# Sliding-window attention followed by a swish feed-forward layer: a second table for the order of all operations, the engine choices, the PSUM slots and the idle products

## The chip, the core and the metric

The kernel runs on one core of a Trainium2 chip. The metric is device microseconds of one execution; lower is better. The core has a matmul engine (PE, with PEld for its weight loads), a vector engine (DVE), a scalar engine (ACT), a general engine (POOL) and a queue that issues most of the DMA transfers (SP). Each engine works through its own list of instructions in order and waits where an input or a buffer is not there yet.

## What is computed

Attention over 4 batches, 8 heads, 768 positions and 64 columns a head, then a feed-forward layer on the 3072 rows that come out of it. Three heads (0, 2 and 6) are causal over all earlier keys. The other five see only the first 4 keys ("sink") and a window of the last 64.

```python
scores = q @ k.T / sqrt(64)              # per batch and head
keep   = causal                          # heads 0, 2, 6
keep   = causal & (is_sink | in_window)  # heads 1, 3, 4, 5, 7
a      = softmax(where(keep, scores, -1e9))
x      = (a @ v).reshape(3072, 512)
h      = x @ w_in                        # 512 -> 2048
g      = h * sigmoid(beta * h)
out    = g @ w_out                       # 2048 -> 512
```

Inputs and output are float32; the products run on bfloat16 copies.

## The kernel before, in words

**Units.** The work is cut into 8 units: batch `b` (0 to 3) by half of the sequence `u` (0, 1), 384 positions each, numbered n = 2b + u. For each unit the kernel does the following; the names are those of the code and of the tiles.

- Loads of q and k (`load_qk`, a transfer of 192 KB for two heads, tiles q2f and k2f; for units 4 to 7 `load_block`, three transfers into a wf tile) and of v (`load_v`, vf or wf).
- Casts to bfloat16 (`cast_qk`, `cast_block` into c; `cast_v` into vb) and shifted or patched copies of v (`shift_v`, `sink_v`: vs, vb; `cast_edge`: VE).
- Transposes of q and k to columns: for units 0 to 3 as products with an identity on PE (`transposes_of`, `transposes`) with a copy out of PSUM (`qk_copy`, tile QK), for units 4 to 7 as DMA transposes (`turn_block`). `kp_copy` and `qd_copy` prepare more copies of k and q (KP, and a k2f tile).
- Scores (`scores`, PSUM tiles sp and b), exponentials on ACT (`exps`, tile es), masks (`masks`), row sums as products with one-hot columns (`sums`, `sums_d`, PSUM tile b) and products with v (`pv`, PSUM tile sp).
- For units 0 and 1 the reciprocals of the sums are spread by products on PE (`recips`, `split`, `spread`, `norm_held`). For units 2 to 7 they are turned and spread by DMA: `sums_copy` moves the sums to tile sc, `sums_turn` transfers them to rec, `recips_d` takes the reciprocal there (DVE RECIPROCAL rec), `spread_w` writes them to device memory (rd), `spread_r` reads them back into tile R, two transfers of 384 KB for an even unit, and for an odd one two of 192 KB, one of 384 KB and a small one. `norm` then multiplies the products with v by R into xT.
- The feed-forward layer: 16 up-steps of four products (`mm1`, xT by w_in into a b bank, 384 columns), a tanh on ACT (`swish_a`, tile t, 2 buffers) and a multiply on DVE (`swish_b`, tile gT), then 48 down-products (`mm2`, gT by w_out, 512 columns) in three groups of 16 with a copy out (`out_copy`, tile osb, 3 buffers) and a store each (`out_store`). The last 128 rows of unit 7 are done in two parts of 384 and 128 columns (`mm2_last`, `last_copy`, `last_store`).

The weights w_in and w_out come in four transfers of 1 MB each into wf (`load_w_in`, `load_w_out`, 3 buffers of wf, shared with the later loads) and are cast by POOL in four pieces each (`cast_w_in`, `cast_w_out`). The up-steps of unit 0 need the first w_in transfer.

**What sets the order.** Every operation is entered once with `plan.add` (1109 of them: engine or engines it may run on, what it needs and gives, which PSUM slot it takes or drops). The entered costs are not used any more: `_Plan.run` goes through the table `SEQUENCE`, which lists the operations' numbers, and emits them one after the other. So each engine's order is the order of its operations in that table. Where an operation may run on several engines, the string `CHOICE` says which ("a" ACT, "d" DVE, "g" POOL). The string `SLOTS` says which of the 4 single PSUM banks (b) or the 2 double banks (sp) an operation takes. `_Ordered` keeps the emitted order.

**Idle products.** `fill` puts products whose result nobody reads ahead of the real ones into a bank that is about to be written: `fill_first` 25 of them at the very start (input blank, an xT tile of zeros), and the table `FILLS` says how many before which operation of the first units (products of blank, or transposes of the identity where the bank is a bfloat16 one).

Of the kernel before, what the change touches and what calls it, by code (L numbers as in the profile page):

```python
# [38 lines left out]


SEQUENCE = [
# [51 lines left out]
]  # L93
CHOICE = (
    "daagaddadadddadaddaddgggdgdddgaaaggggggaaagdddaddaddagddddgaaddgddaaadagddadadagggggadggagdgggagggdd"
    "gaadaaadaaadaaadaadaadaaaada"
)
SLOTS = (
    "0120130120131210031201100312010312132301201031210032103101230012031203120312310231010210310210231021"
    "0301100101201013021302130210130211031001201032100123012301230123001200131230120130123012310021013203"  # L100
    "01130012103210013201320132100023102301231212310231001230123012301230210"
)


# [1 line left out]
    return bass.AP(ap.tensor, ap.offset + offset, [list(ap.ap[0])] + dims)  # L106


FILLS = {24: 4, 28: 8, 32: 1, 36: 1, 45: 5, 51: 7, 54: 5, 60: 1}


class _Ordered:
# [60 lines left out]
def kernel(  # L173
# [1260 lines left out]
    for i, f, e in plan.run():  # L1434
        held["fill"] = FILLS.get(i, 0)
        f(e)
# [35 lines left out]
```

## Time and profile before

| what | us |
|---|---|
| median of 3 runs (lowest to highest) | 229.29 (228.82 to 229.96) |
| span of the profiled execution | 227.1 |
| the median less the span | 2.2 |
| PE busy, share of the span | 220.0 (97%) |
| DVE busy | 152.0 (67%) |
| ACT busy | 144.4 (64%) |
| POOL busy | 97.1 (43%) |

The span goes from the first to the last instruction of one profiled execution; the runs' time contains what lies around it too. The trace has no time of the profiled execution other than its span, so the difference of 2.2 us to the median is taken for what lies around it. A busy PE counts each product from its start to its modelled end, so a short pause between two products does not show as idle; the distance from the start of one product to the start of the next does show it. "L123" in the rows is the line of the recording helper `_Ordered`, the same for all; the tiles tell the operations apart. In a row of the timeline stand the start, the time that the merged instructions took, the engine, the operation, the tile written and those read, the shapes, the count, and in brackets the idle time before it and what ended that.

### The profile page before, as it was taken

To read this page: it belongs to the slowest core of one execution; us is meant where nothing else is said; L and a number is where in the kernel's file an instruction comes from. 1 tells how busy PE (TensorE), PEld (TensorE's weight loads), DVE (VectorE), ACT (ScalarE), POOL (GpSimd) and SP (SyncE) were. 2 spreads that over 40 slices of the span, in tenths; PEclk is the share of its full clock that TensorE was granted. 3 is DMA by queue.
4 is the path that set the end of the run, shared out by engine and by line. 5 is a ranking of instruction groups with operands and counts; after the bars stand their busy time and mean duration, and the time that the engine had idled before them with its cause. 6 is when DMAs were issued, how large, how long until landed. Compare 5 with 4: busy or idle time off the path is not lost.

```text
span 227.1 us, 6564 instructions
## 1 busy us (share of the span) xinstructions
PE 220.0 (97%) x2595; PEld 127.2 (56%) x2595; DVE 152.0 (67%) x391; ACT 144.4 (64%) x244; POOL 97.1 (43%) x238
## 2 busy tenths in 40 slices
PE   7688999999999999999999999999999999999995
PEld 7564567664545565555654665465655555456543
DVE  5787988888292878856862668983796864157700
ACT  6899979886447488616786198318965665118620
POOL 5528966965978108749566293042800000000000
PEclk9999999999999999999999999999999999999999
DMA  6999999998999969999999996947801027021012
GB/s 185 283 321 369 242 343 349 371 335 217 233 205 244 213 131 235 270 176 208 267 219 189 202 214 192 219 26 178 188 0 46 4 89 200 3 92 46 3 46 92
DMA packets 84264, 42.28 MB, mean 186 GB/s; under 512 B 66042, under 2 KB 77002, under 8 KB 84234
## 3 DMA queue, kind: packets, MB, share of 16 engines
q1 hardware_dynamic: 83962, 41.67, 76.7%
q8 instruction: 20, 0.33, 0.6%
q10 hardware_dynamic: 272, 0.20, 0.3%
q14 instruction: 10, 0.08, 0.1%
HBM read 32.27 MB, written 6.37 MB: 170 GB/s over the span
## 4 chain that ended last, share of the span: by engine, by line
PE 87%; DMA 5%; DVE 3%; ACT 2%; SPq 1%; issue 1%; POOL 0%; ACTq 0%
PE b L123 77%; PE sp L123 10%; DMA vf<-in_v_dram 3%; DMA q2f<-in_q_dram 2%; DVE gT L123 1%; ACT t L123 1%; SPq L123 1%; ACT R L123 1%; DVE vs L123 1%; DVE xT L123 0%; ACT vb L123 0%; DVE QK L123 0%; POOL c L123 0%; DVE b L123 0%; DVE lo L123 0%
## 5 line engine op out<-in xcount | busy, mean ns | idle before, releaser
L123 PE MATMUL b<-xT,w_in 128*128 128x384 bf16 x512 | 89.9, 326 | 0.1
L123 PE MATMUL b<-w_out,gT 128*128 128x512 bf16 (+2 forms) x400 | 88.3, 371 | 0.0
L123 DVE SCALAR_TENSOR_TENSOR gT<-t,b 128x384 bf16<-128x384 f32 x128 | 68.5, 551 | 26.2 <-ACT t L123 22.5
L123 ACT ACTIVATE t<-b,beta_h 128x384 f32<-128x384 f32 x128 | 72.2, 586 | 18.3 <-PE b L123 9.7
L123 PEld LDWEIGHTS <-w_in 128*128 128x128 bf16 x512 | 48.6, 98 | 33.4 <-issue 0.6
L123 PEld LDWEIGHTS <-gT 128*128 128x128 bf16 x400 | 37.4, 98 | 40.9 <-issue 0.8
L123 ACT ACTIVATE es<-sp 128x1024 bf16<-128x1024 f32 (+2 forms) x44 | 41.2, 961 | 6.5 <-PE sp L123 6.0
L123 ACT ACTIVATE osb<-b 128x512 f32<-128x512 f32 (+1 forms) x18 | 10.5, 583 | 34.7 <-PE b L123 34.7
L123 DVE TENSOR_TENSOR xT<-sp,R 64x384 bf16<-64x384 f32 (+4 forms) x31 | 16.6, 554 | 12.2 <-PE sp L123 9.2
L123 POOL CAST c<-wf 128x256 bf16<-128x256 f32 x48 | 20.7, 473 | 7.6 <-DMA wf<-in_k_dram 7.4
L123 POOL COPY KP<-QK 128x24 bf16<-128x24 bf16 (+5 forms) x41 | 9.9, 286 | 27.1 <-DMA QK<-c 16.6
L123 PE MATMUL sp<-QK 64*64 64x128 bf16 (+6 forms) x360 | 14.9, 240 | 0.9 <-ACT QK L123 0.8
L123 DVE TENSOR_TENSOR es<-es,mask_s 128x128 bf16<-128x128 bf16 (+8 forms) x34 | 13.0, 402 | 3.8 <-ACT es L123 3.6
L123 PEld LDWEIGHTS <-QK 64*64 64x64 bf16 (+1 forms) x432 | 10.8, 106 | 7.2 <-issue 4.9
L123 DVE TENSOR_TENSOR es<-es,mask_c 128x128 bf16<-128x128 bf16 (+3 forms) x42 | 10.4, 272 | 6.2 <-ACT es L123 6.1
L123 POOL CAST vb<-wf 128x512 bf16<-128x512 f32 x18 | 11.2, 629 | 7.9 <-DMA wf<-in_v_dram 7.8
L123 PE MATMUL sp<-es,vb 128*64 128x64 bf16 (+5 forms) x245 | 13.0, 233 | 0.3 <-ACT es L123 0.3
L123 ACT COPY sc<-b 128x384 f32<-128x384 f32 x5 | 2.4, 479 | 15.7 <-PE b L123 15.7
L123 DVE TENSOR_SCALAR osb<-b 128x512 f32<-128x512 f32 (+1 forms) x7 | 4.7, 667 | 11.3 <-PE b L123 11.3
L123 PEld LDWEIGHTS <-vb 128*64 128x64 bf16 x257 | 11.6, 111 | 0.7 <-issue 0.3
L123 POOL CAST w_in<-wf 128x512 bf16<-128x512 f32 x16 | 9.4, 624 | 4.7 <-DMA wf<-in_moe_w_in_dram 4.6
L123 DVE COPY QK<-b 128x384 bf16<-128x384 bf16 (+1 forms) x13 | 8.2, 640 | 4.8 <-PE b L123 4.7
(120 smaller groups left out, 212.1 us busy)
## 6 DMA issues: line engine op xcount, KB each, us to landing
out_dram<-osb SPq DMA_DIRECT2D x23, 256.0 KB, 3.6
wf<-in_v_dram SPq DMA_DIRECT2D x18, 256.0 KB, 5.3
wf<-in_moe_w_in_dram SPq DMA_DIRECT2D x4, 1024.0 KB, 8.5
wf<-in_moe_w_out_dram SPq DMA_DIRECT2D x4, 1024.0 KB
R<-rd SPq DMA_DIRECT2D x9, 384.0 KB, 5.7
q2f<-in_q_dram SPq DMA_DIRECT2D x16, 192.0 KB, 4.1
wf<-in_q_dram SPq DMA_DIRECT2D x12, 256.0 KB, 4.0
wf<-in_k_dram SPq DMA_DIRECT2D x12, 256.0 KB, 3.8
```

Source lines behind the costliest of these rows:

```text
L123: ins = f(*a, **k)
```

## The change

Four tables are replaced; no function is touched, and the operations with their needs are the same.

- `SEQUENCE`: another order of the same 1109 operations.
- `CHOICE`: 60 operations change their engine. ACT has 14 fewer, POOL 6 fewer, DVE 20 more. Of the casts of q and k for units 0 and 1, DVE has 7 instead of 3. From ACT to DVE go three copies of sums (units 2, 5 and 6), the copies of eight output blocks and of the last small part of the output (128 columns), and two casts of constants; from DVE to ACT go two output blocks and the larger last part (384 columns). Some copies out of PSUM into QK change both ways.
- `SLOTS`: other PSUM banks for the new order.
- `FILLS`: the idle products after the first 25 are dealt to other places, 29 in place of 32.

```diff
 SEQUENCE = [
-    0, 2, 467, 477, 482, 478, 14, 12, 484, 4, 6, 483, 485, 8, 486, 464, 1, 3, 470, 80, 469, 28, 82, 26, 29, 27, 10,
...
+    467, 0, 4, 477, 6, 469, 478, 5, 482, 30, 483, 1, 2, 7, 12, 3, 13, 32, 14, 484, 26, 8, 33, 10, 31, 27, 464, 80,
...
 CHOICE = (
-    "daagaddadadddadaddaddgggdgdddgaaaggggggaaagdddaddaddagddddgaaddgddaaadagddadadagggggadggagdgggagggdd"
-    "gaadaaadaaadaaadaadaadaaaada"
+    "gagdadggdggddaadadaaddgdggddddaaddgddgdagdgdddadddaadgdddddaaddddaaaadddgaddadadddggagdgdggdggdggddg"
+    "dddaaadddddaaaddaaddddaadaad"
...
-FILLS = {24: 4, 28: 8, 32: 1, 36: 1, 45: 5, 51: 7, 54: 5, 60: 1}
+FILLS = {24: 3, 28: 3, 30: 7, 45: 3, 51: 3, 54: 5, 76: 3, 104: 2}
```

What this does to an engine is read from its list of instructions. First the SP queue near the start, from the row behind the load of beta (osb) on; six loads of q and k stand ahead of beta there before, and seven now. The loads named q2f and k2f are 192 KB each, those named vf are v for unit 0, wf is the first w_in transfer and those after it. Before:

```order
L123 DMA q2f<-in_q_dram 128x2x192
L123 DMA k2f<-in_k_dram 128x2x192 x2
L123 DMA vf<-in_v_dram 128x8x64 x3
L123 DMA wf<-in_moe_w_in_dram 128x4x512
L123 DMA k2f<-in_k_dram 128x2x192
L123 DMA q2f<-in_q_dram 128x2x192 x3
L123 DMA k2f<-in_k_dram 128x2x192 x2
L123 DMA wf<-in_moe_w_in_dram 128x4x512 x2
```

And now:

```order
L123 DMA q2f<-in_q_dram 128x2x192
L123 DMA k2f<-in_k_dram 128x2x192
L123 DMA q2f<-in_q_dram 128x2x192
L123 DMA vf<-in_v_dram 128x8x64 x2
L123 DMA k2f<-in_k_dram 128x2x192
L123 DMA vf<-in_v_dram 128x8x64
L123 DMA q2f<-in_q_dram 128x2x192
L123 DMA wf<-in_moe_w_in_dram 128x4x512
L123 DMA k2f<-in_k_dram 128x2x192
L123 DMA wf<-in_moe_w_in_dram 128x4x512
```

In front of the first w_in transfer stand 12 loads of q and k on SP where there were 9 (one more is on ACT's queue in both), and the same three of v; between the first and the second w_in transfer stands one such load where there were six.

Next the SP queue around the sums of unit 2: rec<-sc is `sums_turn`, rd<-rec `spread_w`, R<-rd `spread_r`; wf<-in_v is v for unit 3, wf<-in_q and wf<-in_k are the blocks for unit 4, out_dram<-osb are stores. Before:

```order
L123 DMA wf<-in_q_dram 128x8x64 x3
L123 DMA rec<-sc 96x1x32
L123 DMA wf<-in_v_dram 128x8x64 x3
L123 DMA vf<-in_v_dram 10x8x64 x3
L123 DMA rd<-rec 96x32
L123 DMA out_dram<-osb 128x512
L123 DMA wf<-in_k_dram 128x8x64 x3
L123 DMA out_dram<-osb 128x512
L123 DMA R<-rd 64x4x384 x2
```

And now:

```order
L123 DMA wf<-in_q_dram 128x8x64 x3
L123 DMA wf<-in_k_dram 128x8x64 x3
L123 DMA vf<-in_v_dram 10x8x64 x3
L123 DMA rec<-sc 96x1x32
L123 DMA wf<-in_v_dram 128x8x64 x3
L123 DMA rd<-rec 96x32
L123 DMA_TRANSPOSE QK_109<-c 128x8x128
L123 DMA R<-rd 64x4x384 x2
```

The k blocks of unit 4 now stand ahead of the sums, two stores stand behind R, and a DMA transpose for unit 4 stands between rd and R.

Last DVE at the same place, up to the reciprocal of unit 2's sums (RECIPROCAL rec). gT is `swish_b`, QK with k2f are copies for unit 3, KP is `kp_copy`, VE and vs belong to v, es with mask_c is a mask. Before:

```order
L123 SCALAR_TENSOR_TENSOR gT<-t,b_1432 128x384
L123 COPY QK_110<-b_1572 128x2x384
L123 COPY k2f<-QK_110 64x384
L123 COPY k2f<-QK_110 64x256
L123 RECIPROCAL rec<-rec 96x32
L123 COPY QK_110<-b_1609 128x2x384
```

And now, the last twelve rows ahead of it (the copy of the sums, sc, which was ACT's, stands a few rows further up, with a copy into QK, two into k2f and three into KP between):

```order
L123 COPY KP_112<-QK_110 128x6x60
L123 COPY KP_112<-QK_110 128x6x4
L123 COPY KP_112<-QK_110 128x6x6
L123 COPY KP_113<-QK_110 128x6x60
L123 COPY KP_113<-QK_110 128x6x4
L123 COPY KP_113<-QK_110 128x6x6
L123 MEMSET VE 128x224
L123 CAST VE<-vf 30x448
L123 TENSOR_TENSOR es_1_1617<-es_1_1617,mask_c 128x2x128 x2
L123 COPY vs<-vb 64x1024
L123 MEMSET vs 64x128
L123 RECIPROCAL rec<-rec 96x32
```

The reciprocal, which stood right behind two small copies, now stands behind nine copies into KP, two rows for VE, two masks and two rows for vs.

On PE, the row sums of unit 2 stand 27 down-products and four groups of transposes later than before, the first up-step of unit 2 where it was: between the two lie 53 down-products now, and 80 with the four groups before. For unit 7 there are 27 down-products and 13 up-steps between the sums and the unit's first up-step, and 64 and 11 before. The large products (up and down) run in 37 stretches with smaller ones between, and in 39 before.

More of the change, by code (lines that the diff above doesn't have):

```diff
@@ L41 @@
 SEQUENCE = [
[51 rows of a table removed]
[51 rows of a table added]
 ]
 CHOICE = (
-    "daagaddadadddadaddaddgggdgdddgaaaggggggaaagdddaddaddagddddgaaddgddaaadagddadadagggggadggagdgggagggdd"
-    "gaadaaadaaadaaadaadaadaaaada"
+    "gagdadggdggddaadadaaddgdggddddaaddgddgdagdgdddadddaadgdddddaaddddaaaadddgaddadadddggagdgdggdggdggddg"
+    "dddaaadddddaaaddaaddddaadaad"
 )
 SLOTS = (
-    "0120130120131210031201100312010312132301201031210032103101230012031203120312310231010210310210231021"
-    "0301100101201013021302130210130211031001201032100123012301230123001200131230120130123012310021013203"
-    "01130012103210013201320132100023102301231212310231001230123012301230210"
+    "0123001213002110101101211010312010320131012013210101320110201321031203120312031203101201320132310201"
+    "0213101310101332103210320113021103210132110103101201320132013212010101023103130201102302301020132031"
+    "01231010213021032103210131001320131031031023110020320301210302302130130"
 )
```

100 rows, old and new, of the table SEQUENCE are left out of this document.

## Prediction

> **What bounds the kernel now.** I read the page first: shares of the engines, the clock, and what the transfers moved in 40 slices.
>
> ```profile
> span 227.1 us, 6564 instructions
> ...
> PE 220.0 (97%) x2595; PEld 127.2 (56%) x2595; DVE 152.0 (67%) x391; ACT 144.4 (64%) x244; POOL 97.1 (43%) x238
> ...
> PEclk9999999999999999999999999999999999999999
> ...
> GB/s 185 283 321 369 242 343 349 371 335 217 233 205 244 213 131 235 270 176 208 267 219 189 202 214 192 219 26 178 188 0 46 4 89 200 3 92 46 3 46 92
> ```
>
> PE is busy for 220.0 of 227.1 us, at full clock from the first slice on. So an order can win only where PE is idle, 7.1 us in all, or where PE's own work gets shorter. Next the busy time by stretch, in columns PE, PEld, DVE, ACT, POOL, clock, DMA share, GB/s:
>
> ```profile
> 0.00:22.50 22.50, 18.26 (x297) 13.09 (x297) 16.26 (x61) 18.67 (x32) 12.16 (x42) 1.00 0.97 289
> 22.50:224.30 201.80, 201.74 (x2300) 114.12 (x2298) 135.70 (x332) 125.44 (x212) 84.94 (x196) 1.00 0.76 176
> ```
>
> Of the 7.1 us idle, 4.24 lie in the first 22.5 us, where the transfer engines are 97% busy, and 0.06 in the 201.8 us after that; the other 2.8 are the last output's way out. From 22.5 us on PE never waits, so there a new order can only lose, but for shorter PE work. The start can win or lose. Of it I read PE's timeline:
>
> ```profile
> 18.58 0.49 PE L123 MATMUL b<-xT,w_in 128*128 128x384 bf16 x2
> 19.36 0.34 PE L123 MATMUL b<-ident,c 128*128 128x128 bf16 x3 [0.29 <-POOL c L123]
> ...
> 20.10 0.65 PE L123 MATMUL b<-xT,w_in 128*128 128x384 bf16 x3
> 20.59 0.33 PE L123 MATMUL b<-ident,c 128*128 128x128 bf16 x3
> 20.76 0.49 PE L123 MATMUL b<-xT,w_in 128*128 128x384 bf16 x2
> 21.52 0.34 PE L123 MATMUL b<-ident,c 128*128 128x128 bf16 x3 [0.27 <-DVE QK L123]
> ...
> 22.60 0.54 PE L123 MATMUL sp<-QK 64*64 64x64 bf16 x23
> ```
>
> The first up-step starts at 18.58 us; around it stand transposes of unit 1 that wait for their casts. Two up-products take 2 x 0.162 us (worked out below), so PE paused from about 18.91 to 19.36 (0.45) and from 21.09 to 21.52 (0.43). What released the first up-step is in POOL's timeline and SP's, with DVE's for xT:
>
> ```profile
> 17.54 1.17 POOL L123 CAST w_in<-wf 128x512 bf16<-128x512 f32 x2 [2.87 <-DMA wf<-in_moe_w_in_dram]
> ```
>
> ```profile
> 9.44 1.02 SPq L123 DMA_DIRECT2D wf<-in_moe_w_in_dram  x1
> ```
>
> ```profile
> 17.61 1.95 DVE L123 TENSOR_TENSOR xT<-b,R 128x384 bf16<-128x384 f32 x4 [0.40 <-PE b L123]
> ```
>
> The first w_in transfer is issued at 9.44 us and POOL, waiting for it, starts to cast at 17.54: 8.1 us for 1 MB at a time when 283 to 321 GB/s flow, so it stood behind what was queued ahead of it.
>
> **Part A, the start.** Three more q and k loads of 192 KB (0.59 MB) stand ahead of w_in. At the 283 to 321 GB/s of the second and third slice that is 1.8 to 2.1 us: w_in lands at 19.4 to 19.6 instead of 17.5, and two pieces cast in 1.17 put the first up-step at 20.5 to 20.8. How late may it be without loss? PE now does work ahead of it that came behind: by the rows above the transposes and scores from 19.36 to 20.10 (0.74), the transposes from 20.59 to 20.76 (0.17), and about 14 of the 23 small products at 22.60, some 0.2: 1.1 us. The two pauses (0.88) go too, since what they wait for is loaded sooner. So it may start at 18.58 + 1.1 + 0.9 = 20.6. Between 20.5 and 20.8 I take **+0.1**. Bounds: at the first slice's 185 GB/s the three loads cost 3.2 us, which leaves +1.2; at 369 GB/s 1.6 us, which leaves -0.4.
>
> Four casts of q and k more on DVE (0.36 us each by the row in the rivals) lie in 22.50 - 16.26 = 6.2 us of idle DVE, and POOL loses them ahead of its w_in casts; nothing, unless they land just ahead of xT (a rival). Three fewer idle products stand where PE waits anyway: nothing, and if one stood on the path it would save some 0.1.
>
> **Part B, unit 2.** Its row sums come later on PE and its first up-step doesn't. Here is PE after the sums, and the product xT that ends the way:
>
> ```profile
> 55.96 3.63 PE L123 MATMUL b<-w_out,gT 128*128 128x512 bf16 x16
> 59.42 1.17 PE L123 MATMUL b<-ident,c 128*128 128x128 bf16 x18
> 60.43 0.81 PE L123 MATMUL b<-w_out,gT 128*128 128x512 bf16 x3
> ```
>
> ```profile
> 76.65 2.60 DVE L123 TENSOR_TENSOR xT<-sp,R 64x384 bf16<-64x384 f32 x4 [0.65 <-PE sp L123]
> ```
>
> Sixteen down-products take 59.42 - 55.96 = 3.46 us, 0.216 each (and an up-product of 384 columns three quarters of it, 0.162). The room from the sums' end to xT was 76.65 - 55.96 = 20.7 us. It loses 27 x 0.216 = 5.8 and four groups of transposes, 24 products, 18 of which take 1.01 and so all 1.34: **13.5 us** are left. The chain that must fit was, on SP and DVE:
>
> ```profile
> 58.20 0.79 SPq L123 DMA_DIRECT2D rec<-sc  x1
> ...
> 63.73 0.45 SPq L123 DMA_DIRECT2D rd<-rec  x1
> ...
> 67.94 1.34 SPq L123 DMA_DIRECT2D R<-rd  x2
> ```
>
> ```profile
> 61.83 0.39 DVE L123 COPY k2f<-QK 64x384 bf16<-64x384 bf16 x2 [0.91 <-ACT QK L123]
> 62.25 0.35 DVE L123 RECIPROCAL rec<-rec 96x32 f32<-96x32 f32 x1
> 62.52 0.89 DVE L123 COPY QK<-b 128x768 bf16<-128x768 bf16 x1
> 63.44 1.12 DVE L123 COPY KP<-QK 128x360 bf16<-128x360 bf16 x9
> ...
> 66.06 0.38 DVE L123 CAST VE<-vf 30x448 bf16<-30x448 f32 x1
> ```
>
> The tile view gives the way of R from issue to landing, and SP's timeline the price of the DMA transpose that now stands ahead of R:
>
> ```profile
> DMA to landing us min/median/max: 3.4/4.4/5.7
> ```
>
> ```profile
> 81.77 1.26 SPq L123 DMA_TRANSPOSE QK<-c  x1
> ```
>
> Of the DVE work that now stands ahead of the reciprocal nearly all is the stretch from 61.83 to 66.44, 4.6 us with the reciprocal in it; with the copy of the sums (no DVE row shows it; half of QK's 0.89, an estimate: 0.4) and one more mask (0.3, likewise) it ends 5.3 us after the sums. The turn of the sums runs beside it: issued at 58.20, its result was in use at 62.25, at most 4.05 us, so it is not later than DVE. Then rd's issue, 0.45, and the transpose's, 1.26: the first R is issued at 7.0 and the second 0.67 (half of 1.34) later, at 7.7. With 4.4 us to land R is all there at 12.1, with 5.7 at 13.4; the room is 13.5. Should R wait for rd as it did before (63.73 to 67.94 = 4.2 us, with two stores and three loads between, which hide whether it waited), R goes out at 5.3 + 4.2 = 9.5 and 10.2 and is there between 13.9 (the first, at 4.4) and 15.9 (the second, at 5.7). I take the short way and **+0.2**; the ends are 0 and +2.4.
>
> **Part C, units 6 and 7.** The same trip for unit 7, on PE, SP and DVE:
>
> ```profile
> 180.33 1.47 PE L123 MATMUL b<-xT,w_in 128*128 128x384 bf16 x8
> ```
>
> ```profile
> 186.23 1.94 SPq L123 DMA_DIRECT2D R<-rd  x3
> ```
>
> ```profile
> 199.47 2.83 DVE L123 TENSOR_TENSOR xT<-sp,R 64x384 bf16<-64x384 f32 x6 [4.18 <-PE sp L123]
> ```
>
> The room was 199.47 - 180.33 = 19.1 us. It loses 37 down-products (8.0) and gains two up-steps of 4 x 0.162 (1.3): 12.4. The last large R was issued at 186.23 + 1.94 - 0.60 = 187.6, 7.2 us after the sums; one of two stores ahead of it goes (-0.4), and 4.4 to 5.7 us of landing give 11.2 to 12.5. It just fits: **+0.1**, ends 0 and +0.8 (a slow R with the products gT queued behind xT on DVE). Unit 6's trip is cut in the same manner; it gets no term of its own.
>
> **What else moves.** A change between small and large products costs PE about 0.1: twelve up-products from 25.81 need 1.95, and the next row starts 2.05 later.
>
> ```profile
> 25.81 2.12 PE L123 MATMUL b<-xT,w_in 128*128 128x384 bf16 x12
> 27.86 0.36 PE L123 MATMUL sp<-QK 64*64 64x64 bf16 x14
> ```
>
> There are 37 stretches of large products instead of 39: **-0.2**. At the end the last small part goes from ACT to DVE, and the larger part from DVE to ACT, and only the former lies on the path:
>
> ```profile
> 223.43 0.56 DVE L123 TENSOR_SCALAR osb<-b 128x384 f32<-128x384 f32 x1 [7.69 <-PE b L123]
> 224.37 0.28 ACT L123 ACTIVATE osb<-b 128x128 f32<-128x128 f32 x1 [2.94 <-PE b L123]
> ```
>
> ACT took 0.28 for 128 columns; DVE took 0.56 for 384, so between a third of that, 0.19, and 0.56 for 128: between -0.1 and +0.3, and I take 0. The other engine changes (output blocks, three copies of sums, PSUM copies) lie on DVE and ACT, which are idle for 227.1 - 152.0 = 75 and 83 us; they count only where they stand ahead of a link of B or C, and are in those sums.
>
> The sum: 0.1 + 0.2 + 0.1 - 0.2 = +0.2 on a span of 227.1, so 227.3; the median lies 2.2 above the profiled span, so **229.5 us**.
>
> **The rivals.** *R just too late (slower).* One or both of R's trips at units 2 and 7 end behind PE. For it: a single unit already let DVE wait for R, where PE had other work to do:
>
> ```profile
> 98.31 2.83 DVE L123 TENSOR_TENSOR xT<-sp,R 64x384 bf16<-64x384 f32 x6 [2.55 <-DMA R<-rd]
> ```
>
> In the new order the rooms of B (13.5) and C (12.4) are used to the end. Against it: what is queued on PE in front of the first up-step can be reached with the median landing. It decides once R lands over 13.5 us after the sums of unit 2: with rd waited for, 13.9 to 15.9, that is 0.4 to 2.4, and 0.5 at unit 7: about +1.9 in the middle, **231.2 us**, at the worst 232.5.
>
> *DVE and POOL in each other's way (slower).* DVE's casts at the start come in two lengths, one of q and the one of k, of the same shape:
>
> ```profile
> L123 DVE CAST c<-q2f 128x384 bf16<-128x384 f32 x2 | 0.7, 360 | 0.4 <-DMA q2f<-in_q_dram 0.4
> L123 DVE CAST c<-k2f 128x384 bf16<-128x384 f32 x1 | 0.7, 708 | 0.3 <-DMA k2f<-in_k_dram 0.3
> ```
>
> One that meets POOL would be 0.35 us longer. Six casts ahead of xT instead of three, all six doubled, make xT 2.1 us later; xT's four products ended at 19.56 and are needed by 20.6, so 1.1 is left: **230.6 us**. The Trainium skill ("SBUF — State Buffer", section "Who interferes with whom") says that a DVE operation in its two-port mode and a GpSimd operation shut each other out, and the second to issue fully blocks; by that rule each cast on DVE may wait for a POOL cast beside it, which speaks against moving more of them to DVE while POOL casts w_in. The row of 708 agrees, though one cast can't show what made it long; the two of 360 ran free.
>
> *The start gets shorter (faster).* The w_in transfer doesn't queue strictly behind the three loads but shares with them, and the moved products fill idle time. If it lands as before, the first up-step is at 18.58 with 1.1 us done ahead of it and the pauses gone: -2.0, **227.3 us**; half of it is 228.4. For it: 4.24 us idle at the start, of which only 0.88 are in the sum. Against: 8.1 us for 1 MB is the time of a queue.
>
> *No change that shows*: the forecast itself, 229.5, its own range 228.2 to 230.4.
>
> **How the numbers follow.** About 0.5% (1.15 us) is what a measurement of this kernel can tell from no change. Forecast case 0.40; R too late 0.25; DVE and POOL 0.07; shorter start 0.28. Of the last, 0.04 stays above 228.1 (half the gain gives 228.4): faster 0.24, same 0.44, slower 0.32. The range leaves out about a third of the faster case and a quarter of R's, with some tail of the rest 2 in 10: 227.6 to 231.9.
>
> **What would show it.** In the profile after: w_in's first cast on POOL near 19.5 (part A; near 17.5 the third rival); the first up-step near 20.6; PE's idle in the first 22.5 us near 4.2; PE waits on xT at unit 2 or 7 in the list of waits (the first rival), and DVE's idle before xT ended by R; casts c on DVE of 700 ns (the second). The forecast is wrong if PE waits more than 0.3 us in all after 22.5 us, or if PE's busy time is not within 0.5 of 220.0.

## The result and the profile after

The kernel after takes **236.68 us** (median of 4 runs, 236.16 to 239.27) against 229.1: 1.033 times the time of before, interval 1.029 to 1.037. The forecast was 229.5, its range ended at 231.9. Where the runs of a kernel scatter, a ratio here goes by its faster runs unless the text says otherwise. The profiled execution has a span of 234.6 where before had 227.1.

The page of after, the shares and the clock in 40 slices, and then the stretches of the prediction's table (PE, PEld, DVE, ACT, POOL, clock, DMA share, GB/s):

```profile
span 234.6 us, 6546 instructions
...
PE 223.6 (95%) x2592; PEld 129.7 (55%) x2592; DVE 166.5 (71%) x426; ACT 137.9 (59%) x229; POOL 90.8 (39%) x217
...
PEclk9679999999999999999999999999999999999999
```

```profile
0.00:22.50 22.50, 18.29 (x295) 13.70 (x296) 16.66 (x63) 15.18 (x26) 12.84 (x40) 0.85 0.92 281
22.50:231.80 209.30, 205.25 (x2299) 116.03 (x2297) 149.51 (x363) 122.69 (x204) 77.96 (x177) 1.00 0.75 171
231.80:234.60 2.80, 0.04 (x1) 0.00 (x0) 0.29 (x1) 0.00 (x0) 0.00 (x0) 1.00 0.28 94
```

PE now stands for 4.05 us between 22.5 and 231.8, where before had 0.06, and its clock was 0.85 in the first stretch. The tail is the same 2.8 us. In the busy time pauses hide, so I also took each operation on PE from its first product to that of the next, against the quickest of its kind. What after loses more than before by that count:

| stretch (us) | lost more (us) | where |
|---|---|---|
| 0 to 22.5 | 1.6 | the start |
| 22.5 to 80 | 0.5 | small ones |
| 80 to 100 | 1.7 | first up-steps of unit 2 |
| 100 to 120 | 0.9 | sums of unit 4 |
| 120 to 150 | 0.5 | scores of unit 5 and small ones |
| 150 to 170 | 1.6 | first up-step of unit 5, sums of unit 6 |
| 170 to the end | 0.8 | scores of unit 7, up-steps of unit 6 |

Together 7.6 us by this count, for a span that is 7.5 longer. First the start. PE's timeline of after, then the clock by 2.5 us (second column PE's busy time, third from the right the clock), then DVE's and POOL's share of it:

```profile
5.30 0.34 PE L123 MATMUL b<-ident,c 128*128 128x128 bf16 x3 [0.94 <-POOL c L123]
6.45 0.51 PE L123 MATMUL b<-ident,c 128*128 128x128 bf16 x6 [0.81 <-DVE c L123]
...
20.81 0.24 PE L123 MATMUL b<-KP,sel 128*128 128x192 bf16 x1 [0.23 <-DVE KP L123]
...
22.32 0.32 PE L123 MATMUL b<-xT,w_in 128*128 128x384 bf16 x1
```

```profile
5.00:7.50 2.50, 1.37 (x18) 1.10 (x19) 1.47 (x8) 0.67 (x2) 1.48 (x4) 0.96 1.06 339
7.50:10.00 2.50, 2.39 (x26) 1.54 (x28) 2.21 (x10) 1.98 (x5) 1.31 (x6) 0.50 0.97 271
10.00:12.50 2.50, 2.50 (x27) 1.86 (x28) 1.56 (x6) 2.30 (x5) 1.26 (x6) 0.50 0.97 226
12.50:15.00 2.50, 2.44 (x33) 1.51 (x31) 2.47 (x5) 2.04 (x4) 2.42 (x4) 0.67 1.04 250
```

```profile
11.76:20.25 8.49, 7.45 (x163) 5.02 (x164) 8.31 (x21) 6.72 (x12) 4.21 (x10) 0.86 1.02 325
```

```profile
20.03 2.31 POOL L123 CAST w_in<-wf 128x512 bf16<-128x512 f32 x4 [4.03 <-DMA wf<-in_moe_w_in_dram]
```

```profile
12.82 1.51 DVE L123 TENSOR_TENSOR osb<-osb,mask_s 128x768 bf16<-128x768 bf16 x1
...
16.73 0.54 DVE L123 TENSOR_TENSOR osb<-osb,mask_s 128x768 bf16<-128x768 bf16 x1
...
21.24 1.95 DVE L123 TENSOR_TENSOR xT<-b,R 128x384 bf16<-128x384 f32 x4
```

The same stretch of before:

```profile
11.76:20.25 8.49, 7.46 (x169) 4.83 (x166) 7.08 (x19) 7.65 (x13) 3.43 (x8) 1.00 1.04 338
```

PE waits twice for its first casts; then its clock is at half for some 6.8 us (0.2 of the first row, all of the next two, 1.6 of the last). The first up-step comes at 22.32. The w_in transfer is there at 20.03 and its first piece is cast some 0.6 us later, so what held the up-step is the way to xT: DVE is busy for 8.31 of the 8.49 us from 11.76 on, for 7.08 in before, and the chain that ended last runs through DVE alone there, up to KP (the reciprocals that PE spreads for xT), for which PE waits at 20.81. In before PE spreads them from 17.18 on. xT starts at 21.24 without a pause, where in before it started at 17.61 after one.

Second, unit 2: SP, DVE and PE of after.

```profile
66.13 0.76 SPq L123 DMA_DIRECT2D rec<-sc  x1
...
70.76 0.34 SPq L123 DMA_DIRECT2D rd<-rec  x1
71.21 1.35 SPq L123 DMA_TRANSPOSE QK<-c  x1
73.39 2.21 SPq L123 DMA_DIRECT2D R<-rd  x2
```

```profile
65.43 0.56 DVE L123 COPY sc<-b 128x384 f32<-128x384 f32 x1 [2.13 <-PE b L123]
...
80.90 2.60 DVE L123 TENSOR_TENSOR xT<-sp,R 64x384 bf16<-64x384 f32 x4 [3.04 <-DMA R<-rd]
```

```profile
82.10 0.34 PE L123 MATMUL b<-xT,w_in 128*128 128x384 bf16 x1 [0.42 <-DVE xT L123]
82.68 0.32 PE L123 MATMUL b<-xT,w_in 128*128 128x384 bf16 x1 [0.25 <-DVE xT L123]
83.55 6.33 PE L123 MATMUL b<-xT,w_in 128*128 128x384 bf16 x38 [0.54 <-DVE xT L123]
```

The sums are done at 65.4 and R is there at 80.9: 15.5 us. DVE waits 3.04 us for it, PE 1.2 in three pieces, and the rest of the 1.7 in the product ahead. Third, unit 5 and what stands behind it on DVE:

```profile
143.15 1.87 SPq L123 DMA_DIRECT2D rd<-rec  x1
...
147.28 1.97 SPq L123 DMA_DIRECT2D R<-rd  x3
```

```profile
153.82 2.83 DVE L123 TENSOR_TENSOR xT<-sp,R 64x384 bf16<-64x384 f32 x6 [2.36 <-DMA R<-rd]
...
158.61 0.69 DVE L123 TENSOR_SCALAR osb<-b 128x512 f32<-128x512 f32 x1
```

```profile
PE b L123 <- DVE xT L123: 1.6, 4, 0.5
PE b L123 <- DVE es L123: 1.4, 2, 0.7
```

```profile
DVE xT L123 <- DMA R<-rd: 7.8, 4, 3.0
```

In all DVE waits 7.8 us for R in four units (2, 4, 5, 6), where before waited 2.6 in one. What PE waits for is xT and the masks (es) of units 4 and 6, which DVE reaches late.

### The profile page after: what moved, and what is told of

It is laid out like the page before. It is cut to its first block, busy times and chain, and to the rows that moved or that the text cites. A ratio compares the mean times of both kernels' runs of the same rounds, so it can differ in the third digit from the quotient of the medians.

```text
span 234.6 us, 6546 instructions
## 1 busy us (share of the span) xinstructions
PE 223.6 (95%) x2592; PEld 129.7 (55%) x2592; DVE 166.5 (71%) x426; ACT 137.9 (59%) x229; POOL 90.8 (39%) x217
## 4 chain that ended last, share of the span: by engine, by line
PE 61%; DVE 18%; DMA 12%; ACT 4%; issue 2%; SPq 1%; DVEq 0%; ACTq 0%
PE b L123 55%; DMA R<-rd 8%; PE sp L123 6%; DVE es L123 5%; DVE gT L123 4%; DVE xT L123 3%; DMA rd<-rec 2%; ACT t L123 2%; DMA k2f<-in_k_dram 2%; ACT es L123 2%; DVE osb L123 1%; SPq L123 1%; DVE QK L123 1%; DVE c L123 1%; DVE k2f L123 0%
## 5 line engine op out<-in xcount | busy, mean ns | idle before, releaser
L123 PE MATMUL b<-xT,w_in 128*128 128x384 bf16 x512 | 94.0, 326 | 1.9 <-DVE xT L123 1.6
L123 PE MATMUL b<-w_out,gT 128*128 128x512 bf16 (+2 forms) x400 | 91.5, 371 | 0.0
L123 POOL CAST c<-wf 128x256 bf16<-128x256 f32 x48 | 19.4, 441 | 20.6 <-DMA wf<-in_q_dram 10.7
L123 ACT ACTIVATE osb<-b 128x512 f32<-128x512 f32 (+1 forms) x12 | 7.1, 592 | 23.3 <-PE b L123 19.6
L123 DVE TENSOR_SCALAR osb<-b 128x512 f32<-128x512 f32 (+1 forms) x13 | 8.4, 656 | 9.5 <-PE b L123 8.8
L123 DVE TENSOR_TENSOR es<-es,mask_s 128x128 bf16<-128x128 bf16 (+8 forms) x34 | 14.5, 450 | 0.9 <-ACT es L123 0.7
L123 DVE TENSOR_TENSOR es<-es,mask_c 128x128 bf16<-128x128 bf16 (+3 forms) x44 | 13.8, 342 | 0.8 <-ACT es L123 0.6
L123 POOL COPY KP<-QK 128x24 bf16<-128x24 bf16 (+5 forms) x29 | 6.9, 283 | 15.0 <-DMA QK<-c 13.9
L123 PE MATMUL b<-ident,c 128*128 128x128 bf16 x96 | 9.8, 239 | 1.8 <-POOL c L123 0.9
L123 ACT COPY QK<-b 128x384 bf16<-128x384 bf16 (+1 forms) x14 | 8.4, 618 | 5.0 <-PE b L123 5.0
```

The costliest lines, as they stand in the source:

```text
L123: ins = f(*a, **k)
```

## The experiments

My theory after the two traces: the new order has links (what one engine or queue hands to the next) that come just too late, the trips of the sums of units 2 and 5 first, and a start that is late in itself. Rivals: DVE, with 20 operations more, is too full (D); the late start hands its lateness on; the half clock is the start's cost.

Where an order is new, the PSUM banks are dealt anew for it (each time the one that has been free longest). In these kernels the recording helper stands in line 125, not 123. Runs of kernels with the start of after scatter by 0.6 to 3%, and their clock differs (mean clock of a run 0.964 to 1.000); a profile is one of them. What the clock has to do with the scatter stands behind the last run.

**Start of one, rest of the other.**

```diff
+SEQUENCE = AFTER[:290] + [i for i in BEFORE if i not in AFTER[:290]]     # e1, and the reverse: e2
```

> The first 290 operations (to about 28 us) in the order, on the engines and with the idle products of the kernel after, all that follows in the order and on the engines of before. My theory: the start of after costs 1.6 us, almost all of it because PE's clock is halved from 7.4 to 14.1 us, and the rest costs 5.9 in several places behind it; so this gives 229.1 + 1.6 = 230.7 us, with the halved clock in the profile. Rival: the start is harmless once the rest is as before (PE's later work makes up for it, or unit 2 has room): within 0.5 of 229.1.

Measured: 240.70 us, 1.051 (1.047 to 1.054). Neither theory: the cut makes a seam. The first 290 operations aren't the same in the two orders, and up to 80 us PE waits for casts and copies whose turn has moved. But behind 80 us it loses 2.3 us by my count, where before loses 2.0: the rest of before has no stall there although all of it is 12 us late.

> The reverse: the first 290 operations as before, all that follows as in after. My theory: 229.1 + 5.9 = 235.0 us; in the profile full clock, PE stalls of about 1.7 us at the first up-steps of unit 2, 0.9 at the sums of unit 4, 1.5 at units 5 and 6. Rival: the stalls behind 28 us are the late start's own consequence (every link is late because the first ones were): under 231 us.

Measured: 244.33 us, 1.065 (1.062 to 1.068). The seam again, worse (PE waits 7.1 us for one cast). Behind 80 us it loses 10.4 us, where after loses 7.5. So the stalls belong to the later part of the new order and are not handed on by its start.

**More idle products at the start.**

```diff
-FILLS = {24: 3, 28: 3, 30: 7, 45: 3, 51: 3, 54: 5, 76: 3, 104: 2}
+FILLS = {24: 3, 28: 3, 30: 15, 45: 3, 51: 3, 54: 5, 76: 3, 104: 2, 32: 8}
```

> The kernel after with 16 more idle products on PE, 8 more ahead of the second group of transposes (15 for 7) and 8 ahead of the third, in the two pauses from 4.35 to 5.30 and 5.64 to 6.45 us. My theory: the clock stays full and the 1.6 us of the start come back, 235.1 us. Rival: the start is late for its loads, casts and copies and not for the clock: the clock is full but the time 236.7 within 0.5, or the products delay the transposes and it is longer.

Measured: 236.34 us, 1.031 (1.025 to 1.038). The profiled run has the full clock (mean 0.999), and the first up-step comes only 0.4 us sooner (21.89; PE lost 0.4 us less in 22.5 us). So in the place where after's profile has it, from 7.3 to 14.1 us, the half clock cost 0.4 of the 1.6: PE did at leisure what it must else wait for. For the time as a whole the run decides less: its two runs at full clock (mean 0.999 and 1.000) took 235.29 and 235.22 us, near the 235.1 of my theory, and the two others 238.12 and 237.39; after's own four (0.985 to 0.993) lie between 236.16 and 239.27 and aren't ordered by their clock.

**All operations on the engines of before.**

```diff
-CHOICE = AFTER
+CHOICE = BEFORE
```

> The order and idle products of after with every operation on the engine that it had before (60 go back; DVE has 20 operations fewer). Theory D, the load on DVE makes the links late: the stalls at units 2, 4, 5 and 6 go for the most part, 232.5 us or less. Theory O, the order makes them late (sums and masks too near to what needs them): 235.5 to 237.5 us, stalls at the same places.

Measured: 247.66 us, 1.072 (1.064 to 1.079). Taking the 20 operations off DVE makes it worse, with new waits for casts on POOL (2.5 us) and ACT (2.2). Theory D falls in this form: order and choice of engines belong together.

**DVE relieved at the start.**

```diff
 SEQUENCE: operations 62, 22, 93 ahead of 490 (the first w_in cast); 476 behind 75
-CHOICE[62], CHOICE[22], CHOICE[93] = "ddd"
+CHOICE[62], CHOICE[22], CHOICE[93] = "ggg"
```

> The kernel after with DVE relieved at its start: one mask, one shifted copy of v and one cast of q go to POOL, which stands idle from 16.0 to 20.0 us, and one constant mask goes behind xT; 1.6 us of DVE work less ahead of xT of unit 0. Theory: from 11.8 to 20.8 us the chain that sets the first up-step is nothing but DVE, so the first up-step comes 1.0 to 1.5 us sooner than 22.3, and the time falls by about as much, to 235.3 us. Rival: what is late is the loads and the PE with its halved clock; the first up-step moves by less than 0.4 us and the time stays at 236.7.

Measured: 239.34 us, 1.037 (1.030 to 1.044). Not confirmed. POOL is slow at what it was given:

```profile
16.17 1.49 POOL L125 TENSOR_TENSOR es<-es,mask_c 128x256 bf16<-128x256 bf16 x1
17.72 2.08 POOL L125 COPY vs<-vb 64x512 bf16<-64x512 bf16 x3
```

On DVE these had taken 0.27 and 0.63 (the copies as two). But most of the delay of the first up-step, 24.27 for 22.32, is PE's, as DVE, PE and the clock show:

```profile
20.76 0.27 DVE L125 TENSOR_TENSOR KP<-lo,KP 128x192 bf16<-128x192 bf16 x1
```

```profile
22.44 0.34 PE L125 MATMUL b<-KP,sel 128*128 128x192 bf16 x1
```

```profile
19.84:22.44 2.60, 2.60 (x46) 2.43 (x45) 1.55 (x5) 1.22 (x3) 2.58 (x5) 0.50 1.08 373
```

DVE has KP ready at 21.03, 0.3 us later than in after, but PE takes it up 1.4 us after that. It is still at the products with v, which take 2.60 us at half clock (from 19.84) where after did them at full clock in 1.48 (from 19.10). So here the half clock lies on the path and costs over 1 us. That DVE is the chain of after's start stands on the rows above; whether a lighter DVE would have helped, this run can't show.

**All trips of the sums put ahead.**

```diff
 SEQUENCE: 210, 211, 212 (sums of unit 2) ahead of 567; 213 ahead of 189; 214 behind 252; 215 behind 237
 SEQUENCE: 317 behind 316; 318 ahead of 298; 319 ahead of 377; 320 behind 377 (unit 4); 367 ahead of 416 (unit 5)
```

> The kernel after with the trips of the sums through DMA put ahead: at unit 2 the sums 1.7 us sooner on PE, the reciprocal three copies sooner on DVE; at unit 4 the turn of the sums, rd and R ahead of loads and stores on SP (the turn 8 us sooner); at unit 5 rd ahead of a load. Nothing else is moved. Theory: DVE's 7.8 us of waiting for R fall to under 2, the stalls at the first up-steps of units 2 and 5 and at the sums of unit 6 go, and with them 1.3 + 0.6 + 0.9 us: 233.9 us. Rival: PE's stalls there come from the load on DVE and from POOL beside it, the waits for R only stand in time that DVE has to spare: over 236 us.

Measured: 237.89 us, 1.037 (1.032 to 1.042). DVE's waits for R fall as expected, and the loss at 80 to 90 us goes from 1.8 to 0.6. But new waits stand in the list:

```profile
DVE xT L125 <- DMA R<-rd: 2.7, 3, 1.2
```

```profile
PE sp L125 <- POOL VE L125: 0.8, 1, 0.8
...
PE sp L125 <- DMA QK<-c: 0.8, 1, 0.8
```

The loads and DMA transposes that now stand behind the trips on SP come late in their turn. The whole time says less than these waits: up to unit 2 this run has the order of after, yet its profile has the first up-step at 24.84.

**Trips, start, idle products and sums of unit 4 together.** The edits of e3, e5 and e6, and one more:

```diff
 SEQUENCE: 315 (sums of unit 4) behind 707
```

> The edits of the two runs ahead of it together, the 16 more idle products in the first pauses, and the sums of unit 4 on PE four down-products groups later, behind their masks. If the causes add up: 236.7 - 1.3 - 2.8 - 0.4 - 0.9 = 231.3 us. If they stand in each other's shadow: 233 or more.

Measured: 236.78 us, 1.033 (1.027 to 1.039), no better than after. The stalls at units 2 and 5 are gone (0.1 and 0.3 lost at 80 to 90 and 150 to 160 us), 2.1 at 100 and 1.4 at 130 us have come. As the other branch of the expectation has it, they stand in each other's shadow.

**Before without the idle products ahead of the first transposes.**

```diff
-FILLS = {24: 4, 28: 8, 32: 1, 36: 1, 45: 5, 51: 7, 54: 5, 60: 1}
+FILLS = {45: 5, 51: 7, 54: 5, 60: 1}
```

> The kernel before without 14 idle products, those ahead of the first transposes (4, 8, 1 and 1). Theory, from the run with more of them: PE's clock is halved for some 6 us, yet the products done at half rate mostly fill time in which PE waits for casts and loads, so the time grows by less than 1 us (229.1 to 230.1). Rival: in this order the start has less to wait for and half the clock costs 2 us or more: over 231.

Measured: 229.28 us, 1.001 (0.998 to 1.004): no change. The clock column reads 1.00 from the start, but ahead of the first change on record it can't be taken at its word, as three transposes of this run and of before show:

```profile
6.85 0.50 PE L125 MATMUL b<-ident,c 128*128 128x128 bf16 x3
```

```profile
6.34 0.34 PE L123 MATMUL b<-ident,c 128*128 128x128 bf16 x3
```

Products of 128 columns start 107 ns apart in this run up to 11.8 us and 56 ns apart behind that; in before the change comes at 4.9 us. So the start ran at half rate for 7 us longer, as expected, the first up-step came at 19.52 for 18.58, and the time doesn't show it. In before these idle products, and that half clock, cost nothing that can be seen.

**Cut where both orders have done the same 504 operations.**

```diff
+SEQUENCE = AFTER[:504] + BEFORE[504:]     # e9; e10 the reverse; CHOICE likewise
```

> Both orders have the same 504 operations in their first 504 places (to the fourth up-step of unit 2, about 82 us), so they can be cut there without a seam. Here the first 504 in the order, on the engines and with the idle products of after, the rest as before. By the lost time of PE in the two profiles (before 82 us after loses 1.6 at the start, 0.4 up to 50 us and 1.8 at unit 2 more than before) it gives 229.3 + 3.8 = 233.1 us, and behind 82 us no stalls beyond those of before. Rival: the second half of before makes up for it: under 231.5.

Measured: 1.016 (1.005 to 1.027), the lowest run 232.43 us and the median 235.59, with part of every run at half clock. From 110 us on it loses what before loses (1.5 and 1.4 us by the count).

> The reverse: the first 504 operations as before, the rest in the order and on the engines of after. By the same account (0.8 at the sums of unit 4, 0.4 at 120 us, 1.5 at units 5 and 6, 0.8 behind) 229.3 + 3.7 = 233.0 us, with DVE's waits for R at units 4, 5 and 6 as in after. Rival: these stalls only hand on the lateness of the first half, under 230.5.

Measured: 233.96 us, 1.019 (1.011 to 1.027), nearly all at full clock. The halves cost 1.6 and 1.9%, each with an interval of about one per cent to either side; so they agree with the 3.3% of after, but no more closely than that. The place of this half's loss is clear, SP, DVE and PE of this run:

```profile
138.62 1.03 SPq L125 DMA_DIRECT2D rd<-rec  x1
...
141.76 1.99 SPq L125 DMA_DIRECT2D R<-rd  x3
```

```profile
149.17 2.83 DVE L125 TENSOR_TENSOR xT<-sp,R 64x384 bf16<-64x384 f32 x6 [2.83 <-DMA R<-rd]
...
153.97 0.69 DVE L125 TENSOR_SCALAR osb<-b 128x512 f32<-128x512 f32 x1
```

```profile
152.38 0.32 PE L125 MATMUL b<-xT,w_in 128*128 128x384 bf16 x1 [0.64 <-DVE xT L125]
...
154.71 0.81 PE L125 MATMUL b<-xT,w_in 128*128 128x384 bf16 x4 [1.79 <-DVE osb L125]
```

PE waits 0.64 (and 0.4 in the product ahead) for xT, and then 1.79 for a bank that a DVE copy of unit 4's output frees. This copy and three masks stand behind xT in after and ahead of it in before.

**R without the sums.** R is read from q, so the output isn't scaled by the sums.

```diff
-        src = x.rd[:]
+        src = q
 SEQUENCE: spread_r of each unit ahead of its sums_turn
```

> The kernel after with R read from device memory that needs no sums (the input q), in the same transfers, each ahead of the turn of its unit's sums on SP; the turn, the reciprocal and rd stay. The output is not scaled by the sums then. So DVE never waits for R while the queues carry the same. Theory: the late R causes the stalls at units 2, 5 and 6 (1.7 + 0.6 + 0.9): 233.5 us. Rival: DVE and SP are so full that other links come late in its place, as when the trips were put ahead: over 235.5.

Measured: 241.89 us, 1.052 (1.045 to 1.060). A miss, by the experiment's own fault, as SP and DVE show:

```profile
84.19 2.58 SPq L125 DMA_DIRECT2D R<-in_q_dram  x3
...
87.50 1.79 SPq L125 DMA_DIRECT2D rec<-sc  x2
```

```profile
92.17 0.35 DVE L125 RECIPROCAL rec<-rec 96x32 f32<-96x32 f32 x1 [4.50 <-DMA rec<-sc]
```

R has one buffer. R of unit 3 waits on SP until unit 2 has used it, holds the turn of unit 3's sums behind it, and DVE stands 4.5 us at the reciprocal. It leaves the question open and shows the mechanism again.

**The order of the second half on the engines of before.**

```diff
+SEQUENCE = BEFORE[:504] + AFTER[504:], CHOICE = BEFORE     # e12
```

> As the run with the first half of before and the second of after, but the 19 operations of the second half that changed their engine back on the engine of before: the order alone. Theory O, the order makes the links late: within 1 us of that run. Theory D, the work added to DVE does: under 231.

Measured: 236.65 us, 1.030 (1.023 to 1.037), 2.7 us more than with the engines of after. The engines of before don't bring the time back, so theory D falls here too, without the start in the way; nor is it within the 1 us of theory O.

**The work behind xT, R ahead, the sums alone, the start alone.** The last four.

```diff
 e13: e10 with ob.4.0, M.6.3.0, M.6.0.1, M.6.3.1 (DVE) ahead of xT of unit 5
 e14: e10 with rd and R of unit 5 ahead of the load of three (416, unit 7) on SP
 e15: BEFORE with the sums of unit 2 behind ten groups of down-products, its trip behind them
 e16: AFTER[:237] + the rest of BEFORE
```

> The run with the second half of after, and in it on DVE the copy of unit 4's first output block and three masks of unit 6 ahead of xT of unit 5, as in before, instead of behind it. R of unit 5 stays late (DVE waits 2.8 us for it). Theory: of the 3.0 us that PE stands at 151 to 156 us, 1.8 are its wait for the bank that this copy frees, and these go; the 1.05 at the first up-step stay: 233.5 - 1.9 = 231.6 us. Rival: they are the same wait seen twice, and the time stays over 233.

Measured: 233.71 us, 1.017 (1.012 to 1.023), against 233.96 for e10. PE's wait of 1.79 is gone, as expected:

```profile
150.19 0.68 DVE L125 TENSOR_SCALAR osb<-b 128x512 f32<-128x512 f32 x1
...
151.62 2.84 DVE L125 TENSOR_TENSOR xT<-sp,R 64x384 bf16<-64x384 f32 x6
```

But xT comes 2.45 us later than in e10, since DVE does the copy and the masks first, and the first up-step's stall grows from 1.05 to 1.5 us. The loss there falls from 3.2 to 1.8 us; a stall of 1.0 at unit 2, which e10's profile lacks and two other runs with this cut have, takes most of that back. So PE's wait for the bank is shown to come from this place of the copy, and the whole time doesn't move by it.

> The run with the second half of after, and in it on SP rd and R of unit 5 ahead of a load of three transfers (unit 7) and a store instead of behind them; DVE as in after. Theory: R lands by 145 instead of 149.2 us, DVE doesn't wait for it, both stalls at 151 to 156 us go (3.0 us): 230.7 us. Rival: the load that stands behind now is late for unit 7, or DVE is late without R: over 232.5.

Measured: 239.64 us, 1.041 (1.034 to 1.048). The rival holds: DVE doesn't wait for R of unit 5 any more, but the load for unit 7 goes out at 143.3 instead of 134.4, its transposes at 155.8 instead of 145.8, and PE waits for them:

```profile
161.72 0.61 PE L125 MATMUL sp<-QK 64*128 64x384 bf16 x8 [3.65 <-DMA QK<-c]
```

> The kernel before with the row sums of unit 2 on PE behind ten groups of down-products and four of transposes (7.4 us later), the copy, the turn, the reciprocal, rd and R behind them in turn; all else as it was. Theory: R takes the 15.5 us of after from the sums to landing, so it lands at 78.9, xT comes 2.3 us later than at 76.65, PE stalls at the first up-step of unit 2 for about 1.9 us: 231.1 us. Rival: the room of 13 us is enough where DVE and SP are those of before: within 0.5 of 229.2.

Measured: 233.22 us, 1.014 (1.007 to 1.020). The mechanism is confirmed, at a higher price than the 231.1 us expected:

```profile
79.86 2.60 DVE L125 TENSOR_TENSOR xT<-sp,R 64x384 bf16<-64x384 f32 x4 [3.33 <-DMA R<-rd]
```

```profile
81.06 0.32 PE L125 MATMUL b<-xT,w_in 128*128 128x384 bf16 x1 [1.18 <-DVE xT L125]
```

The profiled run has a span of 229.9, 2.8 more than before, and PE loses 2.5 us at the two operations at which after loses 1.7. The later sums of unit 2 alone, on the engines of before, do this.

> The first 237 operations (to about 23 us) in the order, on the engines and with the idle products of after, the rest as before; the two orders differ there in six operations, none of them on PE. Theory: the start alone costs 1.6 us at half clock as in after's profile, up to 3 where the halved clock lasts longer: 231 to 232 us. Rival: the rest of before hands it back: under 230.

Measured: 240.39 us (235.94 to 242.82), 1.049 (1.041 to 1.057), and 1.029 by the lowest run, the profiled one. More than expected even there: it loses 9.2 us in the first 22.5 (before 5.0) and 2.4 more up to 60, at casts on POOL above all. No later part of before hands it back. How much of it is the start's own and how much the cut's, this run can't tell; e9, with the same start and a cut that lies far behind it, has a run of 232.43.

**The clock over these profiles.** From 18.0 to 21.5 us the granted clock is 1.00 in the profiles of after and e3, and their first up-steps come at 22.32 and 21.89. In those of e1, e5, e6, e7, e9, e11 and e16, which all begin as after does (e5 and e7 with a few operations moved), it is 0.50, and the first up-step comes between 24.27 and 25.65. So the start of after is no fixed loss of 1.6 us, and a late half clock goes with 2.0 to 3.3 us more. The rows of e5 show over 1 us of this as PE's own; the rest isn't shown, for these seven kernels also have their banks dealt anew and the others not.

## Why the prediction was wrong

- **What bounds the kernel.** PE idle only at the start, and behind 22.5 us an order that can only lose: this held. I then priced only the three places at which the room between sums and xT had changed. That selection is the main failure: of 7.5 us only the 1.7 at unit 2 came from a place whose term could hold it.
- **Part A.** W_in landed at 20.0 for the 19.4 to 19.6 forecast, so the queue was read rightly. The step that failed is that four casts more on DVE "lie in 22.50 - 16.26 = 6.2 us of idle DVE" and cost nothing: the idle time was a sum over the stretch, and from 11.76 on DVE has none left. The chain to xT (KP at 20.75, in before at 17.12), not w_in, set the first up-step, at 22.32 instead of 20.5 to 20.8. The two pauses of before went, as said, and two of 0.94 and 0.81 came sooner in the program. The term was +0.1 with a bound of +1.2; by the count it is 1.6. The prediction also has no term for the clock: it read a full clock from the first slice on, where the spacing of the products says from 4.9 us on, and put the fewer idle products at nothing. In after's profile the clock fell, which by e3 cost 0.4 us; in e5's it cost over 1.
- **Part B.** The chain was right and so was the long way of it, 13.9 to 15.9 us; the step that failed is the choice of the short way. In the sum R doesn't wait for rd, though 4.2 us stood between them in before. In after R's issue follows rd's by 73.39 - 70.76 = 2.6 us, the two issues took 2.2 for 1.34, and landing was 15.5 us behind the sums. The cost was 1.7 (e15 alone: 2.5) within the bound of 2.4.
- **Part C.** Unit 7 just fitted, as forecast. Of units 4 to 6 I said that they have no term. Unit 5's room had grown by two groups of three down-products; but its copy of the sums now stood on DVE behind xT of unit 4, which waited 1.87 us for its own R, and its rd on SP behind two loads (reciprocal done at 140.3, rd issued at 143.15). The trip took from 129.9 to 153.8, and PE paid at xT and at the masks of unit 6 behind it. "They count only where they stand ahead of a link of B or C" failed there.
- **The sums of unit 4**, 0.9 us, weren't in any case. They stand directly behind their masks, and these run beside POOL's casts and take longer.
- **The tail** was right (0.29 for 0.28 us). The switches' -0.2 can't be seen under the rest.
- **The rivals.** R just too late was the right mechanism, at units 2 and 5 instead of 2 and 7, priced at 1.9 and given 0.25. DVE and POOL in each other's way: the casts weren't doubled as a rule, but other DVE operations were: the mask at 12.82 took 1.51 us beside a POOL mask (12.64 to 13.91) and 0.54 at 16.73 with POOL idle. Over the whole span the operations that DVE has in both kernels took 165.0 us for 157.9 by my count. The Trainium skill ("SBUF — State Buffer", section "Who interferes with whom") says that a DVE operation with two SBUF inputs contends with a GpSimd one that reads SBUF; these rows agree. What share of the loss it is was not tried by itself. The shorter start didn't come.

What stays open: the start's 1.6 us are placed (DVE's chain, in a profile whose half clock came early) but not undone by any run; what the clock adds to the time of the other runs is not settled; and the stalls of 0.3 to 0.5 us behind 100 us are counted, not explained one by one.

## What to carry to other kernels

Where one engine is full and the others feed it through queues that run in order, an order is a set of a dozen links that must each be in time; read the time to spare of each link in the trace before (here R landed ahead of its use in all units but one), not only of those that the change visibly tightens. A share of idle time over a stretch is no room for a moved operation: the room is what lies idle ahead of the next link on that engine. And a late link was not mended here by letting it pass others on a full queue (e6, e7, e14): what it passed was the next late one. The half clock, too, cost what lay on the path while it lasted: nothing that shows in e8, 0.4 us at the first up-step of after, over 1 in e5.

## What the runs showed of the hardware

- PE's granted clock fell to 0.50 for some 6.8 us after three microseconds (4 to 7 us) in which PE was busy for 0.35, 0.34 and 0.55 of each; in before, with 0.94, 0.71 and 0.68, it stayed at 1.00. The Trainium skill ("TensorE: Matmul & The Clock Gate", "Part 1: The HAM clock gate") states the half rate and a window of about 3.4 us; the trace agrees with both, 6.8 being two of these.
- Sixteen more idle transposes of the identity kept the clock at full rate in that run's profile (e3).
- POOL took 1.49 us for a mask that took DVE 0.27, and 2.08 for three shifted copies, which DVE did as two in 0.63, beside a busy DVE (e5).
